# First query load on ScalarE's queue, six instead of nine leading zero products, the gate's "+1" on GpSimd, and a redrawn instruction order

## The chip, the cores and the metric

The kernel runs on one core of a Trainium2 chip. A core has a matrix engine (TensorE, PE in the profile), a vector engine (VectorE, DVE), a scalar engine with table functions (ScalarE, ACT), a general engine (GpSimd, POOL) and a queue engine that mostly issues transfers (SyncE, SP). Each runs its own list of instructions in order; they wait for each other by semaphores. ACT can issue transfers too. The metric is the device time of one execution in microseconds (us). Shorter is better.

## The reference

Two stages follow each other. The first is attention with soft-capped scores over 8 batches, 12 heads, 448 positions and 64 values per head:

```python
scores = scale * np.matmul(q, k.transpose(0, 1, 3, 2))
scores = cap * np.tanh(scores / cap)                     # cap = 30
attn = np.exp(scores - max);  attn /= attn.sum(-1)
x = (attn @ v)  ->  [8, 448, 768]
```

The second takes x (448 x 768 per batch) through a mixture of four attention experts, two of which are chosen for each position:

```python
logits = x @ w_gate;  topk = the two largest of four;  w = softmax of the two
for e in range(4):
    q, k, v = x @ wq[e], x @ wk[e], x @ wv[e]            # 64 wide each
    a = softmax(causal(scale * q @ k.T))
    out += (e in topk) * w_e * (a @ v @ wo[e])
```

Products run in float16 with float32 accumulation; inputs and the output are float32.

## The kernel before

The first stage goes by pairs of heads: 48 pairs p, six to a batch. For a pair, `load` (L471) brings q, k and v from memory: `kf` and `vf` (the first 384 positions), `qf` (all 448), and `ktf` and `vtf`, the last 64 positions, in two transfers of half a tile. The first two pairs are loaded one at a time, the later ones two at a time. `cast` (L618) turns them to float16: for pair 0 k on ACT, q on DVE and the rest on POOL. `tr` (L672) transposes q and k on PE and copies the result from a PSUM bank to `qk` (L695, L699 and L724 for pair 0, L715 for the others). `fill` (L764) makes the scores of one pair in three parts, Y1, X and Y2 (PE lines L752 and L762), into three X banks and two Y banks; `tanh` (L798, instruction at L805) reads each part on ACT, and `expo` (L811, L817) takes one exponential over the whole pair. `pv` (L821; L832 and L839) multiplies with v, DVE divides by the sums (L860, L863), and `xt` (L868) transposes the result into `xT`, the input of the second stage.

The second stage goes by batch, and its work is put between that of the pairs of the next batches: `b_v` (L939) makes v and the logits, `b_gate`, `b_gate1`, `b_gexp` and `b_gate2` (L999 to L1062) work out the gate on POOL and DVE, `b_qk` (L964) projects q and k, `b_mask` (L1064) spreads the choice of experts, `b_score` (L1093 to L1127) makes the expert scores in the X banks and their exponential on ACT (L1122), `b_pv`, `b_ot` and `b_wo` (L1162, L1193, L1222) finish the batch and store it. The last batch has an ending of its own (`last`, L1319; `last2`, L1467), in which many PSUM copies (`evac`, L375 and L381) may go to DVE or ACT. The gate's weights are e/(1+e) and 1/(1+e): `b_gexp` makes e on POOL, `b_gate2` adds 1 (L1056) and takes the reciprocal (L1057) on DVE, and POOL goes on.

The order on each engine is not the program's. `Graph.solve` (L132) is a list planner that runs before the kernel is built: it knows an assumed duration for each operation, a due time worked back from the fixed sequence of ACT (the tanh and exponential instructions), and due times given by hand (`due=(ref, t)`, t us after an ACT instruction). At each step it takes, on the engine that is free first, the ready operation with the least due time. In each 4 us of the plan a number from `SEEDS` (L23, 78 of them) shifts the due times by a pseudo-random amount of up to `JIT`/2. A transfer has an assumed time on the wire (`wire`).

At the start, PE has nothing to do until the first data come. `NWARM` (9) products of zeros, 512 columns each, are issued ahead (L1544), and `NFILL` (30) of 128 columns fill gaps. One small exponential on ACT (L1547) brings the table in early. In order, SP issues k and q of pair 0, k and q of pair 1, then the tails of pair 1, while ACT issues the two `ktf` transfers of pair 0. `tr_first_tails` (L718, L721) transposes pair 0's `ktf` part. Each transfer takes one of eight semaphores in turn, so that the ninth waits until the first has landed.

Of the kernel before, what the change touches and what calls it, by code (L numbers as in the profile page):

```python
# [10 lines left out]
AF = mybir.ActivationFunctionType  # L11
# [10 lines left out]
JIT = 0.549  # L22
SEEDS = (0, 277, 719, 88, 790, 157, 709, 606, 285, 730, 63, 826, 999, 577, 0, 998, 560, 424, 0, 0, 0, 0, 0, 618, 784, 951, 0, 460, 25, 911, 435, 331, 710, 235, 192, 243, 759, 815, 762, 59, 135, 842, 518, 725, 260, 0, 0, 0, 737, 833, 0, 852, 0, 951, 0, 877, 795, 0, 495, 199, 407, 374, 655, 0, 288, 645, 0, 0, 872, 410, 701, 204, 988, 494, 733, 571, 666, 645)  # L23
TWIRE = 0.1
BEGIN = {"POOL": 0.8, "DVE": 0.9, "SP": 0.8, "ACT": 0.8, "PE": 1.25}
NWARM = 9
KEEP = 8
# [3 lines left out]
KD = 34  # L31
NFILL = 30

# [18 lines left out]
class Graph:  # L52
# [79 lines left out]
    def solve(self, when, banks, lent):  # L132
# [44 lines left out]
        while len(order) < n:  # L177
            best = None
            for e, rs in ready.items():
                if not rs:  # L180
                    continue
                c = [(est(o, e), o) for o in rs if e == o.eng or not left]
                if not c:
                    continue
                t0 = min(x[0] for x in c)
                if t0 >= INF or (best is not None and t0 >= best[0]):
                    continue
                def rank(x):
                    u = x[1]
                    if u.name[:4] == "gexp":  # L190
                        return -INF, 0.0, 0
                    d = u.due + lag if u.first or left < TAIL else max(u.due + lag, t0 + 1.12)
                    d -= 0.211 * (u.grp is not None and not u.opens and left >= TAIL)
                    k = SEEDS[int(t0 / 4.0)] if t0 < 4.0 * len(SEEDS) else 0
                    if k:
                        d += ((u.idx * 40503 + k * 9973) % 1009 / 1009.0 - 0.5) * JIT
                    return d - 2.0 * (u.half == 1 and half == 1), u.due, u.idx

                near = t0 + (0.003 if left >= TAIL else SWITCH + 0.02)
                t, o = min((x for x in c if x[0] <= near), key=rank)  # L200
                early = e == "POOL" and t < HEAD
                if (e in ("PE", "DVE") or early) and not o.first:
                    for t2, u in c:
                        if u.first and u.due + lag < t + o.occ + 0.047 and t2 < t + (
                                o.occ if early else max(SWITCH + 0.01, min(o.occ, 0.25))):
                            t, o = t2, u
                            break
                if best is None or t < best[0]:
                    best = (t, e, o)
# [64 lines left out]
def kernel(  # L274
# [196 lines left out]
    def load(p, n):  # L471
# [13 lines left out]
        def tail(eng, dst, src, g):  # L485
# [3 lines left out]
        nc_eng = nc.sync  # L489
        sp(lambda: full(kf[s][:, d], k[b, h, 0:KM], KC), w=w("kf"), name=f"ldk{p}", wire=0.82 * n)  # L490
        sp(lambda: nc_eng.dma_start(qf[s][:, d], q[b, h].rearrange("h (p c) d -> p h (c d)", c=QC)),
           w=w("qf"), name=f"ldq{p}", wire=0.935 * n)

        def tail_(nm, t, src, z):
            eng, e = (nc.scalar, "ACT") if p == 0 and nm == "ktf" else (nc.sync, "SP")
            for g in range(2):
                sp(lambda g=g: tail(eng, t[s][:, dp], src, g), w=[(nm, x, g) for x in key],
                   r=[(z, s)], name=f"ld{nm[:2]}{p}", eng=e, wire=0.165 * n)

# [439 lines left out]
    def b_v(b, ref):  # L939
        x = b % 2  # L940
        for n in range(4):
            g = Group(AUX + XB, 1.8)
            w = WIN[n]
            for j0 in (0, 2, 4):
                def mm(g=g, w=w, j0=j0):
# [7 lines left out]
                   [("vps", b, n)], g, occ=0.22, name=f"v{b}_{n}",  # L953
                   due=(ref, 4.048 + 1.4 * n))
            lo = 64 if n == 3 else 0
# [8 lines left out]
    def b_qk(b, ref):  # L964
        x = b % 2
        for r in range(2):
            for which in "kq":
                g = Group(AUX + XB, 2.4)
                w2 = (wq2 if which == "q" else wk2)[r]
                for j in range(NDC):  # L970
                    def mm(g=g, w2=w2, j=j, which=which):
# [9 lines left out]
                        [(which, b, r)], g, name=f"{which}{b}_{r}",  # L981
                        due=(ref, 12.09 + 5.11 * r + 1.8 * (which == "q")))
                if which == "k":
# [61 lines left out]
    def b_gexp(b, m=4):  # L1045
        x = b % 2
        e = g_e[x][:, 0:m]
        g_(b, lambda: nc.gpsimd.tensor_tensor(e, eul[:, 0:m], e, ALU.pow), [(b, "e"), "eul"],
           ["e"], 1.05, 1.18)

    def b_gate2(b, m=4):
# [3 lines left out]
        e, w0 = g_e[x][:, w], g_w0[x][:, w]  # L1055
        dve(0.11, lambda: V.tensor_scalar_add(w0, e, 1.0), [(b, "e")], [(b, "w0")], lat=0.17)  # L1056
        dve(0.1, lambda: V.reciprocal(w0, w0), [(b, "w0")], [(b, "w0")], lat=0.18)  # L1057
# [484 lines left out]
    for i in range(NWARM + NFILL):  # L1542
# [3 lines left out]
            ["warmps"], gw, due=0.0 if i < NWARM else None, name="fill")  # L1546
    act(0.25, lambda: nc.scalar.activation(rcb[0], warm[:, 0:4].rearrange("p (n o) -> p n o", o=1),  # L1547
                                          AF.Exp), ["warm", "ident"], [("rcb", 0)])
    load(0, 1)
    load(1, 1)  # L1550
    for p in range(NPV):
# [13 lines left out]
        for what in order:  # L1565
            if what == "Y2" and p:
# [3 lines left out]
                pv(p - 1)  # L1570
                xt(p - 1, (ACTS["Y1", p], 4.601))
                if p % HP == 0 and p < NP:
# [15 lines left out]
                if p in exps:  # L1588
                    bb, s = exps[p]
                    b_pv(bb, s)  # L1590
                    if s == 1:
                        b_ot(bb)
                        b_wo(bb, ACTS["Y1", p], *((14.83, 1.8) if bb < LB - 1 else (10.566, 0.5)))
            fill(p, what)
# [68 lines left out]
```

## Time and profile before

| | |
|---|---|
| median of 3 runs | 310.02 us (309.29, 310.02, 310.08) |
| the profiled execution | 309.16 us, of it 307.4 us from its first to its last instruction |
| ACT busy | 290.8 us (95%) |
| PE busy | 280.5 us (91%) |
| DVE busy | 216.0 us (70%) |
| POOL busy | 181.4 us (59%) |
| first tanh (L805) on ACT begins at | 7.03 us |
| moved by transfers | 51.98 MB |

Rows of groups and of the timeline begin with the line of the kernel, engine, operation and tiles; `out<-in`, with partitions x elements. In a timeline the first number is the start in us from the beginning of the span, the second the time to the end of the last of the instructions that the row takes together (x3: three of them), and a bracket tells how long the engine was idle ahead of it and what released it. "SPq" and "ACTq" are the issue of a transfer by these engines; a transfer's "time to landing" counts from its issue.

### The profile page before, as it was taken

Reading aid. Unit: us, or ns where it says so; the run is one execution under the profiler, and the core shown is the slowest. Engines: PE = TensorE matmul, PEld = TensorE weight load, DVE = VectorE, ACT = ScalarE, POOL = GpSimd, SP = SyncE. Lnnn points to the kernel's source line nnn. Section 1 sums busy time; section 2 is a strip of 40 time slices with the busy share of each in tenths; the row PEclk is TensorE's granted clock in tenths of the full one; section 3 lists DMA queues with packets and bytes.
Section 4 is the critical chain, followed back from the end, with each engine's and each line's share of the span. In section 5 each row is a group of like instructions: output and inputs, shape, how many; then the busy total and the mean of one; then the engine's idle time right before and its main releaser. Section 6 shows DMA issues by size and latency. Waiting matters only on the chain.

```text
span 307.4 us, 8998 instructions
## 1 busy us (share of the span) xinstructions
PE 280.5 (91%) x3504; PEld 188.2 (61%) x3504; DVE 216.0 (70%) x660; ACT 290.8 (95%) x245; POOL 181.4 (59%) x502
## 2 busy tenths in 40 slices
PE   8787679999999999999999999999999989999992
PEld 4454446576655766667566676567665766577761
DVE  2363656477679867796866887787768765787882
ACT  3999999999999999999999999999999999999671
POOL 7883436499788572984649873946585413720320
PEclk9997999999999999999999999999999999999998
DMA  6997999899991798249975593186127600422136
GB/s 168 263 213 178 271 277 257 235 238 243 252 240 47 224 265 234 69 130 269 250 195 135 149 320 95 43 248 175 18 43 163 159 8 20 122 72 79 34 144 217
DMA packets 82075, 51.98 MB, mean 169 GB/s; under 512 B 42736, under 2 KB 78320, under 8 KB 82032
## 3 DMA queue, kind: packets, MB, share of 16 engines
q1 hardware_dynamic: 81728, 51.18, 63.7%
q8 instruction: 27, 0.44, 0.6%
q10 hardware_dynamic: 304, 0.23, 0.2%
q14 instruction: 16, 0.13, 0.1%
HBM read 36.19 MB, written 11.01 MB: 154 GB/s over the span
## 4 chain that ended last, share of the span: by engine, by line
PE 53%; ACT 30%; DVE 8%; POOL 5%; issue 2%; DMA 1%; DVEq 0%; ACTq 0%; POOLq 0%
ACT yp L805 15%; ACT yp L817 12%; PE A L974 7%; PE A L839 6%; PE Y L752 6%; PE A L947 4%; PE X L1113 4%; PE A L1234 4%; PE A L832 3%; PE A L1172 2%; PE A L878 2%; PE A L678 2%; DVE ob L381 2%; ACT pP L1122 2%; PE X L762 2%
## 5 line engine op out<-in xcount | busy, mean ns | idle before, releaser
L817 ACT ACTIVATE yp<-yp 128x3136 f16<-128x3136 f16 (+4 forms) x51 | 139.8, 2744 | 0.0
L805 ACT ACTIVATE yp<-Y 128x896 f16<-128x896 f32 (+2 forms) x100 | 96.2, 962 | 1.6 <-PE Y L752 1.6
L805 ACT ACTIVATE yp<-X 128x1344 f16<-128x1344 f32 (+2 forms) x50 | 65.9, 1318 | 0.1
L839 PE MATMUL A<-v,yp 128*128 128x65 f16 x1116 | 55.9, 194 | 0.0
L839 PEld LDWEIGHTS <-yp 128*128 128x128 f16 x1116 | 49.0, 98 | 4.9 <-issue 2.9
L832 PE MATMUL A<-vtz,yp 128*128 128x130 f16 x186 | 41.5, 223 | 10.0 <-ACT yp L817 5.4
L863 DVE TENSOR_TENSOR xk<-A,rca 128x256 f16<-128x256 f32 (+1 forms) x96 | 39.7, 415 | 2.8
L860 DVE RECIPROCAL rca<-A 128x4 f32<-128x4 f32 (+1 forms) x96 | 17.2, 179 | 25.6 <-PE A L839 24.1
L638 POOL CAST q<-qf 112x512 f16<-112x512 f32 x44 | 26.6, 613 | 13.6 <-DMA qf<-in_q_dram 6.6
L664 POOL CAST v<-vf 128x384 f16<-128x384 f32 x48 | 24.4, 514 | 11.2 <-PE A L839 7.1
L381 DVE COPY ob<-A 128x384 f32<-128x384 f32 (+1 forms) x52 | 28.1, 552 | 3.9 <-PE A L1234 2.8
L832 PEld LDWEIGHTS <-yp 128*128 128x128 f16 x186 | 18.1, 97 | 20.0 <-ACT yp L817 11.2
L1187 DVE SCALAR_TENSOR_TENSOR oB<-A,rcb,mw 128x256 f16<-128x256 f32 x54 | 25.3, 479 | 1.4
L715 DVE COPY qk<-A 128x960 f16<-128x960 f16 x33 | 21.0, 653 | 7.2 <-PE A L678 6.7
L752 PE MATMUL Y<-qk 64*128 64x448 f16 x136 | 24.9, 361 | 0.8 <-ACT yp L805 0.4
L1234 PE MATMUL A<-wo,oT 128*128 128x384 f16 x108 | 24.3, 326 | 0.8 <-DVE ob L381 0.3
L1197 POOL TENSOR_TENSOR oS<-oB,oB 128x512 f16<-128x512 f16 x14 | 16.1, 1153 | 14.4 <-DVE oB L1187 10.4
L1172 PE MATMUL A<-vB,pP 128*128 128x260 f16 x135 | 22.8, 274 | 1.0 <-DVE qk L715 0.7
L947 PE MATMUL A<-wvg,xT 128*128 128x260 f16 x168 | 23.0, 274 | 0.2
L678 PE MATMUL A<-ident,q 112*128 112x112 f16 x192 | 20.2, 212 | 2.3 <-DVE q L638 0.8
L623 POOL CAST k<-kf 128x384 f16<-128x384 f32 x33 | 16.6, 512 | 9.7 <-DMA kf<-in_k_dram 6.0
L887 DVE COPY xT<-A 128x448 f16<-128x448 f16 (+1 forms) x48 | 18.0, 377 | 4.8 <-PE A L878 4.5
(231 smaller groups left out, 587.3 us busy)
## 6 DMA issues: line engine op xcount, KB each, us to landing
qf<-in_q_dram SPq DMA_DIRECT2D x23, 448.0 KB, 6.3
kf<-in_k_dram SPq DMA_DIRECT2D x23, 384.0 KB, 5.7
vf<-in_v_dram SPq DMA_DIRECT2D x23, 384.0 KB, 5.1
out_dram<-ob SPq DMA_DIRECT2D x21, 384.0 KB, 3.3
ktf<-in_k_dram SPq DMA_DIRECT2D x46, 32.0 KB, 5.0
vtf<-in_v_dram SPq DMA_DIRECT2D x46, 32.0 KB, 4.5
out_dram<-ob SPq DMA_DIRECT2D x6, 192.0 KB, 3.3
ob<-in_moe_wv_dram SPq DMA_DIRECT2D x2, 384.0 KB, 5.0
```

The lines of the kernel that those rows point to most:

```text
L381: (nc.scalar.copy if o.eng == "ACT" else nc.vector.tensor_copy)(dst(), src())
L638: e(q16[i], qf[s][:, h].rearrange("p h (c d) -> p c h d", c=QC))
L678: nc.tensor.transpose(ps[:, 0:S].rearrange("m (g c t) -> m c g t", c=QC, t=16)[:, c], q16[i][:, c, :, :].rearrange("p h d -> p (h d)"), id ...
L752: nc.tensor.matmul(dst[:, g, o], kT[r, 128 * (c + 1) : 128 * (c + 2)], t[r, qs], start=True, stop=True,)
L805: ACTS[what, p] = act(c_act(n * (b - a)), lambda: nc.scalar.activation(y[:, a:b, 0:n], src[:, 0 : b - a, 0:n], AF.Tanh, scale=isc / capf), ...
L817: act(c_act(n * (b - a), False), lambda a=a, b=b, n=n: nc.scalar.activation(y[:, a:b, 0:n], y[:, a:b, 0:n], AF.Exp, scale=capf), ks, ks, f ...
L832: nc.tensor.matmul(ps[:, n, :, :], y[:, 2, w : w + 128], vtz[u], start=(n == 0), stop=False, skip_group_check=True,)
L839: nc.tensor.matmul(ps[:, n, h, :], y[:, SLOT[c][h], w : w + 128], v16[u][:, h, c, :], start=False, stop=(c == 2), skip_group_check=True,)
L863: dve(c_dve(128 * m), lambda g=g, i=i, rc=rc, m=m: nc.vector.tensor_tensor(xk[p % NXK][:, 2 * i : 2 * i + m, :, :], view(g)[:, 0:m, :, 0:D ...
L947: nc.tensor.matmul(bank(g)[:, 0 : E * Dh + E], xT[x][:, j, w : w + 128], wvg[:, j, :], start=(j == 0), stop=(j == NDC - 1),)
L1172: nc.tensor.matmul(bank(g)[:, 0 : E * (Dh + 1)], pB[pi][:, o : o + 128], vB[x][:, c, :, :], start=(t == 0), stop=(t == len(cs) - 1),)
L1234: nc.tensor.matmul(bank(g)[:, 0 : D // 2], oT[x][:, n // 2, r, n % 2, :], wo2[r][:, c0:c1], start=(r == 0), stop=(r == 1),)
```

## The change

Five things change, all of them in the text of the program; the planner then draws a new order for the whole kernel.

1. Pair 0's q is issued on ACT's queue; pair 0's two `ktf` transfers go from ACT's to SP's queue. The planner's assumed times on the wire for pair 0 are smaller.
2. 6 instead of 9 long zero products ahead, and 42 instead of 30 short ones. The small exponential at the start does not wait for `ident` any more, and its assumed duration is 1.5 us.
3. The "+1" of the gate goes from DVE to POOL.
4. Due times of the second stage's projections, of its output product and of `xt` change, and so do two small tolerances of the planner.
5. The 78 numbers in `SEEDS` are others.

```diff
-SEEDS = (0, 277, 719, 88, 790, 157, ...
+SEEDS = (0, 0, 719, 433, 75, 538, ...
...
-NWARM = 9
+NWARM = 6
...
-NFILL = 30
+NFILL = 42
...
-                near = t0 + (0.003 if left >= TAIL else SWITCH + 0.02)
+                near = t0 + (0.008 if left >= TAIL else SWITCH + 0.02)
...
-                        if u.first and u.due + lag < t + o.occ + 0.047 and t2 < t + (
+                        if u.first and u.due + lag < t + o.occ + 0.052 and t2 < t + (
...
-        sp(lambda: full(kf[s][:, d], k[b, h, 0:KM], KC), w=w("kf"), name=f"ldk{p}", wire=0.82 * n)
-        sp(lambda: nc_eng.dma_start(qf[s][:, d], q[b, h].rearrange("h (p c) d -> p h (c d)", c=QC)),
-           w=w("qf"), name=f"ldq{p}", wire=0.935 * n)
+        q_eng, qe = (nc.scalar, "ACT") if p == 0 else (nc.sync, "SP")
+        sp(lambda: full(kf[s][:, d], k[b, h, 0:KM], KC), w=w("kf"), name=f"ldk{p}",
+           wire=0.82 * n if p else 0.35)
+        sp(lambda: q_eng.dma_start(qf[s][:, d], q[b, h].rearrange("h (p c) d -> p h (c d)", c=QC)),
+           w=w("qf"), name=f"ldq{p}", wire=0.935 * n if p else 0.35, eng=qe)
...
-            eng, e = (nc.scalar, "ACT") if p == 0 and nm == "ktf" else (nc.sync, "SP")
             for g in range(2):
-                sp(lambda g=g: tail(eng, t[s][:, dp], src, g), w=[(nm, x, g) for x in key],
-                   r=[(z, s)], name=f"ld{nm[:2]}{p}", eng=e, wire=0.165 * n)
+                sp(lambda g=g: tail(nc.sync, t[s][:, dp], src, g), w=[(nm, x, g) for x in key],
+                   r=[(z, s)], name=f"ld{nm[:2]}{p}", wire=0.165 * n if p else 0.1)
...
-                   due=(ref, 4.048 + 1.4 * n))
+                   due=(ref, 4.367 + 1.4 * n))
...
-                        due=(ref, 12.09 + 5.11 * r + 1.8 * (which == "q")))
+                        due=(ref, 14.952 + 5.133 * r + 1.8 * (which == "q")))
...
+        g_(b, lambda: nc.gpsimd.tensor_scalar(g_w0[x][:, 0:m], e, 1.0, None, ALU.add), [(b, "e")],
+           ["w0"], 0.19, 0.34)
...
-        dve(0.11, lambda: V.tensor_scalar_add(w0, e, 1.0), [(b, "e")], [(b, "w0")], lat=0.17)
...
-    act(0.25, lambda: nc.scalar.activation(rcb[0], warm[:, 0:4].rearrange("p (n o) -> p n o", o=1),
-                                          AF.Exp), ["warm", "ident"], [("rcb", 0)])
+    act(1.5, lambda: nc.scalar.activation(rcb[0], warm[:, 0:4].rearrange("p (n o) -> p n o", o=1),
+                                          AF.Exp), ["warm"], [("rcb", 0)])
...
-                xt(p - 1, (ACTS["Y1", p], 4.601))
+                xt(p - 1, (ACTS["Y1", p], 4.838))
...
-                        b_wo(bb, ACTS["Y1", p], *((14.83, 1.8) if bb < LB - 1 else (10.566, 0.5)))
+                        b_wo(bb, ACTS["Y1", p], *((14.625, 1.8) if bb < LB - 1 else (10.566, 0.5)))
```

In the order that results, SP issues k of pair 0, the two `ktf` of pair 0, k and q of pair 1, the two `ktf` of pair 1, and then k and q of pairs 2 and 3 ahead of any v. On PE, pair 0's q transposes stand right behind its k transposes, and pair 0's `ktf` transpose (L721 before) stands behind both, with one more zero product between it and the first scores.

## The prediction

> **What bounds the kernel now.** I read the page first, then the busy time by stretches, then ACT's waits, and then the first ten and the last twenty us of the timeline.
>
> ```profile
> span 307.4 us, 8998 instructions
> PE 280.5 (91%) x3504; PEld 188.2 (61%) x3504; DVE 216.0 (70%) x660; ACT 290.8 (95%) x245; POOL 181.4 (59%) x502
> 0.00:7.03 7.03, 5.74 (x34) 2.75 (x34) 2.26 (x9) 2.41 (x4) 5.26 (x28) 1.00 0.61 166
> 7.03:286.00 278.97, 259.38 (x3286) 174.78 (x3285) 199.72 (x600) 277.80 (x216) 171.27 (x465) 0.99 0.66 171
> 286.00:307.40 21.40, 15.39 (x189) 10.65 (x186) 14.02 (x52) 10.58 (x26) 4.88 (x9) 0.95 0.42 142
> ACT yp L805 <- PE Y L752: 1.6, 2, 1.4
> ACT pP L1122 <- PE X L1113: 0.8, 2, 0.5
> ACT qB L381 <- PE X2s L1327: 1.8, 1, 1.8
> ACT pP L1385 <- PE A L1375: 1.5, 2, 1.2
> ```
>
> The rows of stretches give length, then busy time of PE, weight loads, DVE, ACT and POOL, the granted PE clock, the transfer engines' share and GB/s. There are three stages. In the head, 7.03 us, ACT waits for the first scores. In the middle, 278.97 us, ACT is busy for 277.80: only 1.17 us are idle, of which 0.2 (1.6 less the 1.4 of the first tanh) and 0.8 have a named cause. In the ending, 21.4 us, no engine is full. So a change that adds no work to ACT can win only from the head, from 1.17 us, and from the ending; it can lose anywhere. Head and middle add up: ACT's list is the same in both orders up to the ending.
>
> The head row by row:
>
> ```profile
> 0.79 1.20 ACTq L487 DMA_DIRECT2D ktf<-in_k_dram  x2
> 0.79 0.46 SPq L483 DMA_DIRECT2D kf<-in_k_dram  x1
> 1.25 3.59 PE L1544 MATMUL A<-warm 128*128 128x512 f16 x8 [1.25 <-DVE warm L507]
> 1.31 0.46 SPq L491 DMA_DIRECT2D qf<-in_q_dram  x1
> 2.02 1.28 ACT L1547 ACT_TABLE_LOAD   x1 [2.02 <-issue]
> 2.82 1.92 SPq L487 DMA_DIRECT2D ktf<-in_k_dram  x3
> 3.45 0.51 ACT L623 CAST k<-kf 128x384 f16<-128x384 f32 x1
> 4.32 0.43 DVE L638 CAST q<-qf 112x512 f16<-112x512 f32 x1 [1.89 <-DMA qf<-in_q_dram]
> 4.63 0.52 PE L688 MATMUL A<-ident,k 128*128 128x128 f16 x3
> 4.95 0.41 PE L1544 MATMUL A<-warm 128*128 128x512 f16 x1
> 5.06 0.29 POOL L659 CAST ktz<-ktf 128x128 f16<-128x128 f32 x1
> 5.41 0.23 PE L721 MATMUL A<-ident,ktz 128*128 128x128 f16 x1
> 5.71 0.36 PE L678 MATMUL A<-ident,q 112*128 112x112 f16 x4
> 5.91 0.72 PE L1544 MATMUL A<-warm 128*128 128x128 f16 x10
> 6.03 0.51 POOL L623 CAST k<-kf 128x384 f16<-128x384 f32 x1 [0.29 <-DMA kf<-in_k_dram]
> 6.63 0.36 PE L752 MATMUL Y<-qk 64*128 64x448 f16 x2
> 7.03 0.92 ACT L805 ACTIVATE yp<-Y 128x896 f16<-128x896 f32 x1 [1.37 <-PE Y L752]
> 7.94 0.66 DVE L715 COPY qk<-A 128x960 f16<-128x960 f16 x1 [0.97 <-PE A L678]
> 9.46 0.36 PE L752 MATMUL X<-qk 64*128 64x448 f16 x2
> 9.87 1.29 ACT L805 ACTIVATE yp<-X 128x1344 f16<-128x1344 f32 x1
> ```
>
> k is cast by 3.96 (3.45 + 0.51) and q by 4.75 (4.32 + 0.43), yet their transposes start on PE at 4.63 and 5.71. In between PE works off zero products (eight in 3.59 us, 0.449 each), and q's transposes stand behind the ninth and behind the `ktf` transpose at 5.41. From q's transposes to the first tanh it is 1.32 us (7.03 - 5.71).
>
> **The head's terms.** Six zero products end at 1.25 + 6 x 0.449 = 3.94, one short one brings it to about 4.05. If k lands as before, its transposes start there instead of at 4.63, and q's follow after the 0.31 to 0.35 that three transposes hold PE (0.52 less overlap): 4.40. q must be cast by then. Its issue moves from 1.31 to 0.79; the load took 3.0 us from issue to cast, so it lands at 3.8 and is cast at 4.23. It now goes beside k from the beginning, so the unfavourable end is no earlier landing at all: 4.32, cast at 4.75, transposes at 4.8. On ACT one issue (0.46 to 0.6) stands ahead of the table load instead of 1.20, so ACT is no later for k. Along this path the first tanh comes at 5.72 (4.40 + 1.32) to 6.12.
>
> What is late next is `ktf`. Its transposes still stand ahead of the first scores on PE, and its two transfers go from 0.79 on ACT to SP, behind k.
>
> ```profile
> qf<-in_q_dram SPq DMA_DIRECT2D x2, 224.0 KB, 3.6
> kf<-in_k_dram SPq DMA_DIRECT2D x2, 192.0 KB, 3.4
> ktf<-in_k_dram ACTq DMA_DIRECT2D x2, 16.0 KB, 3.2
> ktf<-in_k_dram SPq DMA_DIRECT2D x1, 16.0 KB, 3.8
> DMA to landing us min/median/max: 2.9/3.6/4.7
> ```
>
> The last number of a row is the median time to landing; the last row is for all `ktf` transfers of the first 16 us. SP issues them at 1.31 and, at 0.6 each (1.92 / 3, with a wait in it), 1.92. The later one lands between 1.92 + 2.9 = 4.8 and 1.92 + 3.8 = 5.7, and I take the middle, 5.3, since less traffic lies ahead of it than ahead of the 3.8. From there: cast 0.29, 0.06 to PE (5.35 to 5.41), about 0.25 for the transpose and one zero product, 0.40 to the tanh (6.63 to 7.03): 1.0 us. So the first tanh comes at 5.8 to 6.7; I take 6.3, a gain of 0.73 (0.3 to 1.2).
>
> Then pair 1 has to follow. Its first X tanh is 2.84 us behind the first tanh (9.87 - 7.03), so it would be wanted at 9.14. Its k, q and `ktf` are issued later, by two issues of 0.6 less the one of 0.5: 0.7. If the wire and not the issue sets their landing, nothing is lost (pair 0's k was cast 2.66 after its issue, so with a median of 3.4 pair 1's took about 4.2: it waited for the wire); if the whole 0.7 passes through, the copy at 7.94 ends at 9.3 instead of 8.60, and scores and tanh follow 0.8 later (about 0.4 for scores and 0.4 to ACT): 10.0, no gain. With the POOL cast of `ktf` also holding the k cast behind it (6.03 before, 6.1 to 6.8 now) I keep 0.5 of the 0.73, with ends 0 and 1.1. **Head: -0.5.**
>
> **Zero products.** The short ones only fill gaps; 12 more hold PE 0.07 each (0.72 / 10) where it is waiting: nothing while they stand ahead of work that isn't ready. If the data were early, the six ahead of pair 1's part would cost 0.4, and they are behind the first scores.
>
> A row bears on having fewer of them: the PE clock.
>
> ```profile
> 24.00:28.00 4.00, 2.28 (x29) 1.81 (x30) 0.61 (x2) 3.91 (x4) 1.48 (x5) 0.69 1.12 248
> ```
>
> Where PE did 2.28 us of work in 4, the granted clock went to 0.69. In the head it reads 1.00 throughout, in the stretch up to 7.03. With six long products PE may be idle for some tenths between 4.0 and 5.8; by these rows that costs nothing, since PE has idled longer at 1.00. A slow start is part of the second rival and priced there. The Trainium skill, TensorE: Matmul & The Clock Gate, Part 1, states that the clock is let up after about 3.4 us of sustained activity, in a window that runs freely; by that rule a broken first window would leave the first scores at half the clock, and the time would be the second rival's. The row at 24 us agrees that idleness lowers the clock; the head's rows don't show the start of it.
>
> **The gate.** The row of the removed DVE add and the nearest POOL rows:
>
> ```profile
> L1056 DVE TENSOR_SCALAR g_w<-g_e 128x4 f32<-128x4 f32 x7 | 2.7, 387 | 1.2 <-POOL g_e L1048 1.1
> L1027 POOL TENSOR_SCALAR ms<-g_r 128x16 f32<-128x16 f32 x14 | 3.3, 253 | 0.2
> ```
>
> The columns are busy time, mean ns of one, and the idle time before. DVE loses 7 x 0.39 = 2.7 us, POOL gains at most 7 x 0.25 = 1.8 us of its 181. Neither bounds the middle (70% and 59%). The reciprocal now waits in the add's place and 0.1 to 0.25 longer; what is queued behind it on DVE are copies of PSUM banks, for which PE waits. DVE's own wait here was 1.1 us, all of it in one of the seven batches. In the new order one masked q (L992) stands ahead of that wait. Between -0.5 and +0.25 in one place; I take 0.
>
> **The new order of the middle.** Per half pair, between score products into the Y banks, PE's instructions were counted and priced at columns / 2400 + 0.0025 us each (448 columns: 0.19; two such beside each other in the row at 6.63 take 0.36 with latency). Sums over the kernel agree, 233.27 and 233.29 us; the fullest pair holds 5.80 before and 5.75 after. The projections' due time is 2.86 us later, yet q of batch 0 ends half a pair later and batch 1's and 2's by one to two, while expert scores begin in the same half pair or the next. So PE isn't fuller. What can't be read from order is who waits by some tenths. The bounds are -0.94, if all named waits of 1.0 go save 0.06, and +2.4, if one expert exponential in each of seven batches waits the 0.48 of the longest (3.4, less 0.94). It is nearest to what is there, since durations and ACT's list stay: 0.
>
> **The ending.**
>
> ```profile
> 301.72 0.55 DVE L381 COPY kf<-X0s 128x384 f32<-128x384 f32 x1
> 301.90 0.48 ACT L381 COPY kf<-A 128x384 f32<-128x384 f32 x1 [0.50 <-PE A L1300]
> ```
>
> These are the two halves of the last block, side by side on two engines. In the new order both are on DVE, one behind the other: +0.44 (301.72 + 2 x 0.55 against 302.38). Against this two `ob` copies of the same shape and one copy of v leave DVE for ACT, and two small ones come to it: -2 x 0.55 + 0.55 = -0.55 in copies of this shape. Between the two ends I take +0.1; the two waits of 1.8 and 1.2 at its start stay, since the products that they wait for stand at the same places.
>
> **Sum.** 309.16 - 0.5 + 0 + 0 + 0.1 = 308.76 against the profiled execution. That one lies below all three timed runs, and 0.86 below their median; the mean of the four is 309.64, and -0.4 from there is 309.2. I say 309.1, since the head may keep all of its 0.73. The runs of one kernel scatter by 0.8 us here; 0.3% (0.93 us) is about what a measurement of this kernel can tell from no change.
>
> **Rivals.** (1) The order also takes the waits out of the middle: 309.1 - 0.94 = 308.2. For it: the named waits are few; ahead of the longest, PE has about 0.3 us less to do in the new order. Against: nothing in the text aims at these three places. (2) The head's gain is lost on the way, by `ktf` and pair 1's loads landing late, or by a slow PE clock: ten transposes and five score products at half the clock add about 0.5 + 0.3 between the first tanh and pair 1. The time is then that of before with the ending's 0.1: 309.7. For it: the 0.7 later issue. Against: pair 1's copy at 8.60 had 0.8 until its scores. (3) Slower: expert scores come late. Its place is the X banks in each batch (L1113), its point the moment at which q's masked copies are done later than the ACT slot; later due times move that way. If every second of the fourteen waits 0.48, that is 3.4, so 309.1 + 3.4 - 0.94 = 311.6; with half of them 310.4, and I put 311.0. Against: the half-pair counts.
>
> **Chances.** Forecast 0.50 (308.5 to 309.8 by itself, of which nearly half is below 309.09, the 0.3% bound); rival 1 0.16; rival 2 0.16; rival 3 0.18. Faster: 0.24 + 0.16 + 0.02 = 0.42; same: 0.26 + 0.14 = 0.40; slower 0.18. The range leaves out about 0.05 below and 0.12 above: 308.1 to 310.8.
>
> **What would show it.** Right: the first tanh at 6.0 to 6.6, q's cast at about 3.8 to 4.3, the `ktf` cast on POOL after 4.8 directly ahead of the first scores, pair 1's X tanh at 9.1 to 9.7, ACT idle in the middle near 1.2 us, and the last copy on DVE at about 0.5 ahead of the end of copies before. Wrong: a first tanh after 6.8 (`ktf`), before 5.8 (it wasn't on the path), ACT waits for L1113 of more than 2 us, or transfer waits on POOL of 3 us and more in the 20 to 50 us in which transfers are full.

## The result and the profile after

The changed kernel takes 310.55 us (median of 21 runs, 309.55 to 311.47); the kernel before, run beside it, 309.88 (21 runs, 309.00 to 310.39). The ratio is 1.0024, with a 95% interval of 1.0013 to 1.0035: slower by 0.67 us, where 309.1 was predicted. That lies inside the predicted range, but it is a loss where a gain of 0.8 was forecast (309.1 for 309.88). The profiled run of the changed kernel took 311.4, near the slowest of its 21; that of before 309.16, near its fastest. So the two profiles are 2.2 us apart and the medians 0.67: the profiles name the mechanisms, and their sizes are taken from medians below.

First the lines at the top of the page of the changed kernel.

```profile
span 309.7 us, 9017 instructions
PE 281.0 (91%) x3513; PEld 191.3 (62%) x3513; DVE 214.3 (69%) x653; ACT 290.4 (94%) x245; POOL 182.8 (59%) x509
```

ACT's busy time is nearly the same (290.8 before), so the 2.3 us of span are time in which it waits. Three cuts place them: the beginning of pair 1's X tanh, the end of ACT's last large exponential, the end. Busy time by these stretches (columns as in the prediction), for the kernel before,

```profile
0.00:9.87 9.87, 8.53 (x65) 4.50 (x66) 2.91 (x10) 5.25 (x8) 7.63 (x41) 1.00 0.70 198
9.87:286.67 276.80, 257.26 (x3264) 173.64 (x3264) 199.69 (x602) 275.63 (x214) 169.14 (x454) 0.99 0.66 170
286.67:307.40 20.73, 14.72 (x178) 10.04 (x175) 13.38 (x49) 9.91 (x26) 4.64 (x9) 0.95 0.44 147
```

and for the changed one:

```profile
0.00:11.99 11.99, 9.46 (x62) 5.23 (x62) 2.98 (x10) 5.54 (x7) 6.61 (x35) 1.00 0.77 179
11.99:288.37 276.38, 256.63 (x3279) 176.01 (x3278) 198.36 (x595) 275.17 (x213) 171.55 (x467) 1.00 0.69 169
288.37:309.70 21.33, 14.90 (x176) 10.04 (x174) 12.93 (x49) 9.68 (x26) 4.66 (x9) 0.95 0.42 143
```

Head +2.12, middle -0.42, ending +0.60: together the 2.30 of span (these cuts go by spans printed to a tenth; the ending is good to 0.05). In the middle ACT is idle for 1.21 us (276.38 less 275.17), as before for 1.17 (276.80 less 275.63), but 1.0 of it in one place, L1124, and 0.2 ahead of one Y tanh, where before 0.48, 0.28 and 0.18 were in three places; the 0.42 are in its busy time, 275.17 for 275.63, and so are not waits that went. The wait that is new stands ahead of pair 1's X tanh (ACT's waits, in all, times, longest):

```profile
ACT yp L806 <- PE X L763: 1.3, 1, 1.3
ACT pP L1124 <- PE X L1115: 1.0, 1, 1.0
```

The head, in the timeline of the changed kernel:

```profile
4.61 0.43 DVE L639 CAST q<-qf 112x512 f16<-112x512 f32 x1 [2.18 <-DMA qf<-in_q_dram]
4.81 0.51 ACT L624 CAST k<-kf 128x384 f16<-128x384 f32 x1 [2.06 <-DMA kf<-in_k_dram]
5.30 0.29 POOL L660 CAST ktz<-ktf 128x128 f16<-128x128 f32 x1 [1.16 <-DMA ktf<-in_k_dram]
5.38 0.50 PE L689 MATMUL A<-ident,k 128*128 128x128 f16 x3 [1.29 <-ACT k L624]
6.75 0.55 PE L753 MATMUL Y<-qk 64*128 64x448 f16 x2
7.35 0.92 ACT L806 ACTIVATE yp<-Y 128x896 f16<-128x896 f32 x1 [0.96 <-PE Y L753]
8.39 0.85 PE L1546 MATMUL A<-warm 128*128 128x128 f16 x6
9.17 0.55 PE L753 MATMUL Y<-qk 64*128 64x448 f16 x2
10.46 0.66 DVE L716 COPY qk<-A 128x960 f16<-128x960 f16 x1 [2.91 <-PE A L679]
11.30 0.36 PE L753 MATMUL X<-qk 64*128 64x448 f16 x2
11.99 1.29 ACT L806 ACTIVATE yp<-X 128x1344 f16<-128x1344 f32 x1 [1.31 <-PE X L763]
12.53 0.50 PE L1546 MATMUL A<-warm 128*128 128x128 f16 x6
```

Two things differ from before. Pair 0's k is cast at 4.81 instead of 3.45; PE, out of zero products at 4.09, stood still for 1.29. And PE is slow: two products of 448 columns take 0.55 at 6.75 and at 9.17, and only from 11.30 on the 0.36 that the first scores took before (6.63 there). It is about half speed: six products of 128 columns take 0.85 at 8.39 and three 0.53 at 8.07, so three more cost 0.32; from 12.36 on three take 0.33 and six 0.50, and three more cost 0.17. Pair 1's copy, which stands behind these products, comes at 10.46 instead of 7.94. The clock's column (third from the end) shows nothing of it: it reads 1.00 over the whole of that time.

```profile
6.00:9.00 3.00, 3.00 (x23) 1.79 (x21) 1.08 (x3) 2.04 (x3) 2.21 (x12) 1.00 0.89 217
9.00:12.00 3.00, 3.00 (x31) 1.93 (x28) 0.66 (x1) 1.42 (x3) 0.81 (x3) 1.00 1.08 221
```

The column is a default there. The trace's list of clock records begins only where the clock rises, at 10.52 us in the changed kernel and at 5.00 in the kernel before; for the time ahead of its first record the trace has no clock, and the column counts that as full. So the rise can be read from the trace after all, and it fits the durations.

The ending. The last copies and stores of the changed kernel:

```profile
303.09 0.56 DVE L381 COPY kf<-X0s 128x384 f32<-128x384 f32 x1
303.56 0.55 DVE L381 COPY kf<-A 128x384 f32<-128x384 f32 x1
303.80 1.22 SPq L1318 DMA_DIRECT2D out_dram<-kf  x2
```

Measured from the end of the last large exponential, the last copy ends at 15.74 (303.56 + 0.55 - 288.37), before at 15.71 (301.90 + 0.48 - 286.67). Both halves on DVE cost 0.03, not 0.44, since PE's last product ends 0.18 earlier. The 0.6 arise behind all engines, in the transfers. Their share by half microseconds, at the end of before and of the changed kernel (the last two columns are the share of the 16 transfer engines and GB/s):

```profile
305.40:305.90 0.50, 0.00 (x0) 0.00 (x0) 0.00 (x0) 0.00 (x0) 0.00 (x0) 0.50 0.65 258
305.90:306.40 0.50, 0.00 (x0) 0.00 (x0) 0.00 (x0) 0.00 (x0) 0.00 (x0) 0.50 0.00 0
```

```profile
306.70:307.20 0.50, 0.00 (x0) 0.00 (x0) 0.00 (x0) 0.00 (x0) 0.00 (x0) 1.00 0.80 301
307.20:307.70 0.50, 0.00 (x0) 0.00 (x0) 0.00 (x0) 0.00 (x0) 0.00 (x0) 0.78 0.07 25
307.70:308.20 0.50, 0.00 (x0) 0.00 (x0) 0.00 (x0) 0.00 (x0) 0.00 (x0) 0.50 0.05 18
```

Before, all engines stop together. After, a share of 0.05 to 0.07, that is about one of sixteen, goes on alone for about 0.8 us. The view of queues for the last 4 us has a row in the changed kernel that before has not:

```profile
q14 instruction: 1, 0.01, 0.5%
```

One packet of instructions, 0.01 MB, lies 3.2 us ahead of the end among the last stores. In the kernel before, the last such packet lies 8.3 us ahead. That the engine which goes on alone is the one that carried the packet is not recorded.

### The profile page after: what moved, and what is told of

It reads as the page before. It is cut to its first block, busy times and chain, and to the rows that moved or that the text cites. A ratio compares the mean times of both kernels' runs of the same rounds, so it can differ in the third digit from the quotient of the medians.

```text
span 309.7 us, 9017 instructions
## 1 busy us (share of the span) xinstructions
PE 281.0 (91%) x3513; PEld 191.3 (62%) x3513; DVE 214.3 (69%) x653; ACT 290.4 (94%) x245; POOL 182.8 (59%) x509
## 4 chain that ended last, share of the span: by engine, by line
ACT 67%; PE 13%; DMA 6%; POOL 5%; DVE 4%; issue 3%; DVEq 0%; POOLq 0%
ACT yp L806 34%; ACT yp L818 29%; ACT pP L1124 4%; DMA mT<-mB 3%; PE A L948 2%; DMA kd<-kz 1%; DMA kf<-in_k_dram 1%; DVE qm L993 1%; POOL mB L1071 1%; POOL oS L1199 1%; PE Y L753 1%; DVE ob L381 1%; PE A L1546 1%; PE A L840 1%; PE A L1329 1%
## 5 line engine op out<-in xcount | busy, mean ns | idle before, releaser
L818 ACT ACTIVATE yp<-yp 128x3136 f16<-128x3136 f16 (+4 forms) x51 | 142.5, 2797 | 0.0
L806 ACT ACTIVATE yp<-Y 128x896 f16<-128x896 f32 (+2 forms) x100 | 102.0, 1020 | 1.4 <-PE Y L753 1.4
L806 ACT ACTIVATE yp<-X 128x1344 f16<-128x1344 f32 (+2 forms) x50 | 68.7, 1375 | 1.3 <-PE X L763 1.3
L381 DVE COPY ob<-A 128x384 f32<-128x384 f32 (+1 forms) x50 | 26.9, 553 | 3.0 <-PE A L1236 2.2
L1236 PE MATMUL A<-wo,oT 128*128 128x384 f16 x108 | 25.0, 326 | 1.8 <-DVE ob L381 0.8
L948 PE MATMUL A<-wvg,xT 128*128 128x260 f16 x168 | 21.2, 273 | 0.3 <-DVE xT L888 0.3
L1134 POOL TENSOR_SCALAR_AFFINE_SELECT pP<-pP 128x384 f16<-128x384 f16 x14 | 7.4, 525 | 22.5 <-ACT pP L1124 13.3
```

The source lines that it names most:

```text
L381: (nc.scalar.copy if o.eng == "ACT" else nc.vector.tensor_copy)(dst(), src())
L806: ACTS[what, p] = act(c_act(n * (b - a)), lambda: nc.scalar.activation(y[:, a:b, 0:n], src[:, 0 : b - a, 0:n], AF.Tanh, scale=isc / capf), ...
L818: act(c_act(n * (b - a), False), lambda a=a, b=b, n=n: nc.scalar.activation(y[:, a:b, 0:n], y[:, a:b, 0:n], AF.Exp, scale=capf), ks, ks, f ...
L948: nc.tensor.matmul(bank(g)[:, 0 : E * Dh + E], xT[x][:, j, w : w + 128], wvg[:, j, :], start=(j == 0), stop=(j == NDC - 1),)
L1236: nc.tensor.matmul(bank(g)[:, 0 : D // 2], oT[x][:, n // 2, r, n % 2, :], wo2[r][:, c0:c1], start=(r == 0), stop=(r == 1),)
```

## The experiments

Five theories. (1) The new queues make pair 0's k land late. (2) Six long zero products leave PE at half its clock through the head. (4) The ending's 0.6 is that packet of instructions, and its place hangs on how many instructions an engine has (4a: DVE). (5a) The gate's move is free. (3) was that the head is not the cause at all. In every experiment the planner is as it was and only what is emitted differs, so all other orders stay. The kernel before, run beside each group of them, had medians of 309.50 to 309.69, and 309.88 in the first comparison, so a difference of medians across groups is good to some tenths.

**The queues and the zero products, one at a time.**

```
e1   pair 0: k, q on SP; ktf x2 on ACT          (changed kernel, old queues, 6 long)
e2   pair 0: ktf, k, ktf on SP; q on ACT        (kernel before, nearly the new queues, 9 long)
e3   6 -> 9 long zero products, ahead of all    (changed kernel, new queues)
e4   9 -> 6 long zero products, first 3 out     (kernel before, old queues)
```

In e2 one `ktf` is issued ahead of k, which is neither the changed kernel's order nor that of the expectation below: k is issued at 1.43 instead of 0.79, so part of its late landing there is its late issue.

> The changed kernel with the first two `ktf` transfers back on ACT's queue ahead of its table load, and the first q back on SP behind k, as in the kernel before; six long zero products, everything else and every order stay. Theory 1 (k lands late because of the queues): k is cast at about 3.5 instead of 4.81, its transposes start at about 4.1 instead of 5.38, the first tanh at 6.0 to 6.7, pair 1's X tanh at 9.7 to 10.3 instead of 11.99, and the time is 0.5 to 0.9 below the changed kernel's: 309.7 to 310.1. Theory 2 (six long zero products leave PE at half its clock, whatever the queues): products of 448 columns still take 0.55 instead of 0.36 up to about 10 us, pair 1's X tanh stays at 11 or later, and the time stays at 310.3 to 310.6. Theory 3 (the head is not it, the ending's 0.6 is): 310.3 to 310.6 with pair 1's X tanh early.

> The kernel before with the changed kernel's queues alone: the first q on ACT's queue, and on SP k, then the two `ktf` transfers, then pair 1's. Nine long zero products, all orders as before. Theory 1: k is cast at 4.5 or later instead of 3.45, the first tanh at 7.2 to 7.6, pair 1's X tanh at 10.5 to 12 instead of 9.87: 0.6 to 2.0 slower, 310.5 to 311.9. Theory 2: the ninth zero product covers the gap up to 5.2, PE stays at full clock (0.36 for 448 columns), and the time is within 0.3 of before: 309.6 to 310.2.

> The changed kernel with nine long zero products instead of six, three more ahead of all the others; nothing else. Theory 1: nothing changes, since k still lands late: k's transposes at about 5.4, first tanh at 7.3, 310.4 to 310.7. Theory 2: PE comes to full clock before the first scores (0.36 for 448 columns instead of 0.55), pair 1's X tanh at 10.0 to 10.7 instead of 11.99, and the time falls by 0.7 to 1.5: 309.0 to 309.8.

> The kernel before with six long zero products instead of nine (the first three left out); nothing else. Theory 1 as the only cause: k's transposes start at about 4.0 instead of 4.63, the first tanh comes at 6.2 to 6.6 instead of 7.03 and the time falls by 0.3 to 0.7: 309.2 to 309.6. Theory 2: with PE idle between the zero products and the transposes the clock stays at half, 448 columns take 0.55 up to about 10 us, pair 1's X tanh comes at 10.5 to 12 instead of 9.87, and the time rises by 0.5 to 2.0: 310.4 to 311.9.

| run | median (range) | ratio to before, 95% | k cast | first tanh | X tanh, pair 1 |
|---|---|---|---|---|---|
| e1 | 309.26 (308.51 to 311.17) | 1.0004 [0.9984, 1.0023] | 3.51 | 6.60 | 11.61 |
| e2 | 311.96 (309.49 to 314.17) | 1.0062 [1.0042, 1.0081] | 4.42 | 7.21 | 10.04 |
| e3 | 309.53 (309.17 to 309.85) | 0.9993 [0.9985, 1.0002] | 4.62 | 7.14 | 10.36 |
| e4 | 311.25 (310.07 to 311.98) | 1.0047 [1.0028, 1.0065] | 3.67 | 8.41 | 12.19 |

Theory 2 is borne out twice. Three more long zero products, and nothing else, take 1.02 off the changed kernel (310.55 to 309.53; by the ratios to the kernel before, 1.0024 and 0.9993, it is 0.96) and narrow its runs from 1.9 us to 0.7; three fewer cost the kernel before 1.7 (its X tanh, at 12.19, is 0.2 beyond the expected range). Theory 3 falls with that. Theory 1 is right in its mechanism: with the old queues k is cast at 3.51 and 3.67, with the new at 4.62 (e3). What e1's time says is split: its median is 1.29 below the changed kernel's, lower than either theory expected, but its runs fall into two groups, seven at 308.5 to 309.4 and five at 310.2 to 311.2, and the profiled one is of the upper. In that one the old queues buy nothing, since the clock is slow (timeline, and the row of a stretch):

```profile
3.51 0.51 ACT L624 CAST k<-kf 128x384 f16<-128x384 f32 x1
4.07 0.50 PE L689 MATMUL A<-ident,k 128*128 128x128 f16 x3
6.00 0.56 PE L753 MATMUL Y<-qk 64*128 64x448 f16 x2
8.42 0.56 PE L753 MATMUL Y<-qk 64*128 64x448 f16 x2
11.61 1.29 ACT L806 ACTIVATE yp<-X 128x1344 f16<-128x1344 f32 x1 [1.68 <-PE X L763]
3.90:7.26 3.36, 3.13 (x20) 1.28 (x19) 1.70 (x4) 1.26 (x3) 1.89 (x9) 1.00 0.81 222
```

The first tanh was 0.75 earlier than in the changed kernel's profile, and the X tanh of pair 1 still came at 11.61: the gain of the head as the prediction had worked it out was there (6.60, against 6.3 taken), and PE's half clock ate it before pair 1. PE was busy for 3.13 of 3.36 us in that stretch, and the clock rose only at 10.53.

e2 lies just above what theory 1 expected, but not by its mechanism: its X tanh, at 10.04, is only 0.17 late, and the loss is behind. Pair 2's q is cast late too, PE runs dry in one stretch and is at half clock through the next (the issue of k, a row of the timeline, two stretches with the clock in the third column from the end, and, for the second loss, a row of the timeline and one of DVE's waits):

```profile
1.43 0.58 SPq L483 DMA_DIRECT2D kf<-in_k_dram  x1
12.76 0.90 DVE L638 CAST q<-qf 112x512 f16<-112x512 f32 x2 [3.98 <-DMA qf<-in_q_dram]
11.20:14.60 3.40, 1.78 (x17) 0.92 (x17) 1.27 (x3) 3.40 (x3) 2.20 (x15) 0.99 1.01 267
14.60:18.00 3.40, 3.27 (x35) 2.13 (x33) 1.64 (x6) 2.45 (x3) 3.03 (x17) 0.51 1.00 232
275.45 1.02 ACT L1122 ACTIVATE pP<-X 128x1024 f16<-128x1024 f32 x1 [1.96 <-PE X L1113]
DVE qm L992 <- DMA mT<-mB: 1.9, 1, 1.9
```

That costs ACT about 1 us; another 1.5 (1.96 against 0.48 before) is lost at 275.45, behind a masked q that waited for a transfer. Why that transfer was late there was not tried.

**Which of q and `ktf` holds k back, and how many zero products it takes.** a1 puts the two `ktf` behind q on ACT's queue in e3. b1 is e1 with eight long zero products.

> The changed kernel with nine long zero products (309.53, k cast at 4.62 after a wait of 1.86 for its transfer) and with the first two `ktf` transfers on ACT's queue behind q, so that SP has k and then pair 1's loads and only q, not `ktf`, is issued beside k. If it is `ktf`'s small packets right behind k on the same queue that hold k back: k is cast at about 3.5, and k's transposes start as soon as the long zero products end (5.2). If it is q beside k that takes its share of the wire: k stays at 4.4 to 4.8. Since nine long zero products hold PE to 5.2 anyway, the time hardly moves in either case: 309.2 to 309.8, with `ktf` (cast at 5.3 to 6.0) setting the first tanh.

> The changed kernel with the old queues for pair 0 (its runs with six zero products fell into two groups, 308.5 to 309.4 and 310.2 to 311.2, and the profiled one, of the upper group, had PE at half clock up to 10.6) and with eight long zero products instead of six. Theory 2, in the form that the clock comes up at the end of a stretch of about 3.4 us in which PE had no pause: two more long products close the pauses ahead of the first scores, the clock is up by about 7 in every run, and the upper group goes: 308.5 to 309.2 with a scatter under 1 us, X tanh of pair 1 at 9.4 to 10.2. If the two groups have another cause than PE's pauses (transfers that land late), they stay, and the median lies at 309.3 to 310.0.

a1: 309.96 (309.76 to 310.32), 0.4 above e3 and just above what was expected, which is not explained; k is cast at 4.47 although no `ktf` of pair 0 stood on SP. So it is q beside k, not `ktf` behind it; the 4.28 to 4.81 of all seven profiles with q on ACT's queue stand against 3.41 to 3.67 of all ten without. b1: 309.09 (308.85 to 311.66), with k cast at 3.41, scores at 0.36 from 6.15 on and the X tanh at 9.79. Of eleven runs one was above 310, of e1's twelve five; that one, 311.66, is outside the scatter of 1 us that was expected. By medians b1 is 0.44 below e3, by the ratios to the kernel before (0.9998 and 0.9993) it is not: what the old queues are worth beside a full warm-up is not clear of the noise.

**The same kernel again, and one lucky profile.** Three more profiles of e1 (r1, r2, r3), and the changed kernel with seven memsets on DVE that nobody reads, c2, made for the ending.

```
+  for _ in range(7): nc.vector.memset(pad, 0.0)     ahead of DVE's first cast of q
```

> A second look at the changed kernel with the old queues and six long zero products, whose runs fell into two groups. If the groups are the clock's: a time of 308.5 to 309.4 goes with products of 448 columns at 0.36 from about 6.3 on and pair 1's X tanh at 9.3 to 10.0; a time of 310.2 to 311.2 goes with 0.55 up to 10 and an X tanh at 11.5 or later, as in the first profile.

> A third look at the changed kernel with the old queues and six long zero products. A time of 308.5 to 309.4 must go with products of 448 columns at 0.36 before 8 and pair 1's X tanh at 9.3 to 10.2, if the groups are the clock's; with 0.55 up to 10 it must be 310.2 to 311.2. A time of the lower group with the slow clock would refute it.

> As the look before: 308.5 to 309.4 with 0.36 before 8 and an X tanh at 9.3 to 10.2, or 310.2 to 311.2 with 0.55 up to 10.

> The changed kernel with nothing but the seven memsets on DVE. If the ending's part adds to the head's as it did with nine and with eight long zero products (0.68 and 0.64 less): 309.8 to 310.0 instead of 310.55, ending 20.5 after the last exponential, the slow clock up to 10 and the late X tanh (11 to 12) as they were.

r1, r2, r3 took 311.04, 310.84 and 310.56, with 0.55 to 0.60 for two products of 448 columns up to 8.6 and the X tanh at 11.69, 11.20 and 11.46: the upper time with the slow clock, as expected, each time. The lower time was not among them. c2 shows the other state, against what was expected of it. Its head is that of the changed kernel, with six long products and the new queues, and the memsets beside it on DVE:

```profile
4.43 0.51 ACT L624 CAST k<-kf 128x384 f16<-128x384 f32 x1 [1.67 <-DMA kf<-in_k_dram]
4.99 0.34 PE L689 MATMUL A<-ident,k 128*128 128x128 f16 x3 [0.90 <-ACT k L624]
6.40 0.36 PE L753 MATMUL Y<-qk 64*128 64x448 f16 x2
10.10 1.29 ACT L806 ACTIVATE yp<-X 128x1344 f16<-128x1344 f32 x1 [0.38 <-PE X L763]
```

PE stood still for 0.90 here too, yet at 4.99 it is at full speed, three transposes in 0.34 instead of 0.50, and the X tanh comes at 10.10. So nearly the same head has its clock up at 4.08 in one execution and at 10.52 in another, by the first clock record of each trace. Of the seven profiles with six long products one has the rise at 4.08 and six at 9.67 to 10.64; the ten with eight or nine have it at 4.30 to 6.95, that is no later than in the first X scores. By the profiles, then, half clock up to about 10 is usual with six and does not come with eight or nine. How often it comes in the timed runs is not known, since they have no trace; if e1's lower group is the fast clock, it is the more frequent one there. c2's runs, 309.63 (308.38 to 310.69), are 2.3 us wide, those of e1 2.7; those of e3 and p2 below, with nine long products, 0.7 and 0.9. Width alone does not tell the clock: b1, g3 and e2, with eight or nine, are 2.8 to 4.7 wide.

The Trainium skill, TensorE: Matmul & The Clock Gate, Part 1, says that the clock is set by a window of about 3.4 us that runs freely, and so differs from run to run; the trace agrees, with the 3.40 us at 0.51 in e2 and with the two outcomes above. In the clock records the windows can be counted: stretches at half clock in mid-kernel are 3.41 us long, those at full clock whole multiples of that (6.83 in e1, 20.48 before, 296.96 in the changed kernel). Counted back from the rise, c2's window held the six long products, and the changed kernel's, two windows ahead of its rise, did not hold all of them (c2, then the changed kernel):

```profile
0.66:4.08 3.42, 2.84 (x7) 0.89 (x7) 1.18 (x12) 1.49 (x2) 2.75 (x14) 1.00 0.57 135
0.28:3.69 3.41, 2.45 (x6) 0.89 (x7) 0.82 (x5) 1.49 (x2) 2.60 (x16) 1.00 0.42 95
```

So with six products it is the place of the window that decides. But e1's next window, from 3.70 to 7.11, had PE busy for 3.18 and was not enough. Part 4 of the same page of the Trainium skill states that transposes do not count as busy in the same way, which would fit: 1.34 us of e1's window are transposes (eight, from 4.07 to 5.97). Without the transposes the windows sort in all 17 traces: PE was busy for at most 2.58 us where the clock then stayed down and for at least 2.82 in the window at whose end it rose. No run here takes the transposes away.

**The gate.** g3 is e3 with the seven sums back on DVE, b2 is b1 with the same, g2 is the kernel before with the sums on POOL.

```
g3, b2   - nc.gpsimd.tensor_scalar(g_w0[x][:, 0:m], e, 1.0, None, ALU.add)
         + nc.vector.tensor_scalar_add(g_w0[x][:, 0:m], e, 1.0)
g2       the reverse, in the kernel before
```

> The changed kernel with nine long zero products and the gate's seven sums back on DVE, no order changed otherwise: this is the price of the gate's move, against 309.53. Theory 5a: the move costs nothing in the middle, 309.3 to 309.7. Theory 4 about the ending (one transfer of instructions falls 3.2 ahead of the end in all three profiles of the changed order, and 8.4 ahead in those of the old one, and behind it one of the 16 transfer engines finishes the last stores alone, about 0.6 later than the others): if the place of that transfer hangs on DVE's or POOL's count of instructions (7 more on DVE and 7 fewer on POOL, as in the kernel before), it moves away, the ending falls from 21.34 to about 20.75 after the last exponential, and the time is 308.8 to 309.1. If it stays, the count that matters is another engine's or the order's.

> Old queues, eight long zero products and the gate's sums on DVE, all on the changed order: the sum of the two runs beside it. If the head's and the ending's parts add up: the head's gain of the old queues and the ending without the late transfer engine, 307.9 to 308.6; if the ending stays, as the run with eight alone, 308.5 to 309.2.

> The kernel before with the gate's seven sums on POOL, no order changed otherwise: the gate's part alone, in the old order. In the changed order, taking the sums back to DVE cost 1.5 in the median, because DVE then waited 2.1 for POOL there and ACT behind it. In the old order DVE's wait was 1.1, and the reciprocal behind the sum needs the same data, so the wait stays: the middle within 0.3 of 276.80. Theory 4a: with 7 fewer instructions on DVE the transfer of instructions moves from 8.4 to about 3 ahead of the end and the ending grows from 20.73 to 21.2 or more: 310.0 to 310.3 in all. Otherwise 309.4 to 309.9.

g3: 311.06 (310.23 to 314.57), ratio 1.0065 [1.0038, 1.0091], that is 1.5 above e3. b2: 311.93, 2.8 above b1. g2: 308.85 (308.33 to 309.08), ratio 0.9976 [0.9966, 0.9987], 0.65 below before. None of the three times came as expected. Theory 5a falls in both orders: the gate's move is worth 0.65 in the old order and 1.5 to 2.8 in the new, the ending's part below included. Waits in the middle of g3's profile, of DVE and of ACT (in all, times, longest):

```profile
DVE g_w L1051 <- POOL g_e L1049: 2.1, 3, 1.2
ACT yp L806 <- PE Y L753: 3.6, 3, 1.9
```

With the sum on DVE, DVE waits for POOL in three batches; the copies of PSUM banks stand behind it, PE waits for the banks and ACT for PE. In e3 ACT has no such wait for Y in its middle. The profiled run of g3 is one of its slowest, 313.86, and shows why its runs are so far apart: behind the longest of DVE's waits PE stands still for 2.11 us, so that it is busy for 1.30 of 3.41, and the next 3.41 are at half clock,

```profile
165.46:168.87 3.41, 1.30 (x8) 0.55 (x6) 2.86 (x4) 3.41 (x4) 2.41 (x7) 1.00 1.11 320
168.87:172.29 3.42, 3.42 (x34) 2.13 (x33) 1.92 (x6) 2.62 (x3) 0.59 (x3) 0.50 0.72 255
```

and two of ACT's three waits for Y, 0.80 and 1.87, follow at 171 and 175. In the profile of b2, its fastest run (310.63), the clock stays up and the waits for Y come to 1.2. In g2 the middle is 275.99 instead of 276.80. Of ACT's three waits there in the kernel before (0.18, 0.28, 0.48) one is left; the other two are 0.46 of the 0.81:

```profile
ACT pP L1122 <- PE X L1113: 0.5, 1, 0.5
```

**The ending.** p1 is b1, and p2 is e3, with the seven memsets.

> Old queues and eight long zero products on the changed order (309.09 without more), and seven memsets of a scratch tile that nobody reads on DVE ahead of its first cast, where DVE is idle. Gate and orders as in the changed kernel. Theory 4a (the late transfer of instructions hangs on DVE's count of instructions): it moves from 3.2 to about 7.0 ahead of the end, the ending falls from 21.3 to about 20.4 after the last exponential, the middle stays at 276.4 to 277.0, and the time is 308.1 to 308.5, below both kernels. If it hangs on POOL's count, everything stays: 308.9 to 309.3.

> The same seven memsets on the changed kernel with nine long zero products and its new queues (309.53 without them). Theory 4a: 308.5 to 308.9, ending 20.4. Otherwise 309.3 to 309.8, ending 21.3.

p1: 308.45 (307.61 to 309.14), ratio 0.9961 [0.9947, 0.9975]. p2: 308.85 (308.09 to 309.01), ratio 0.9974 [0.9964, 0.9984]. Both came as expected. These are 0.64 and 0.68 below the same kernels without the memsets. c2 is 0.92 below the changed kernel, but its runs mix both states of the clock. The memsets take 0.82 us where DVE is idle:

```profile
2.38 0.82 DVE L1635 MEMSET pad<- 128x2 uint32 x7
```

The time from the last large exponential to the end sorts all profiles: 20.7 to 20.9 in the old order, 21.3 to 21.4 in the eight of the changed order with its own gate, 20.5 in the five with seven more instructions on DVE, memsets or gate sums. In those five the packet lies 6.9 ahead of the end instead of 3.2, in g2, with seven fewer on DVE, 5.7 instead of 8.3. Theory 4a holds in that DVE's number of instructions moves the packet, in both directions, and that the packet's place is worth 0.64 to 0.68 here. It missed by how far in g2: about 3 and an ending of 21.2 or more were expected, and at 5.7 the ending stayed at 20.9. p1 beats both kernels, by 1.05 and 2.1; of the change it has the orders and the gate, with the old queues, eight long zero products and the memsets.

## Why the prediction was wrong, step by step

- **"If k lands as before, its transposes start there" failed.** q was sent on a second queue beside k, and the step asked only whether q would land earlier. k's cast went from 3.45 to 4.81 in the profile, 4.28 to 4.81 over the runs, and a1 shows that q is what it shares with. q gained less than k lost: its cast began at 4.61 in the profile, beyond the unfavourable end, 4.32, and at 3.76 to 4.61 over the seven profiles with q on ACT's queue, against 4.29 to 4.61 in the ten without. `ktf` came at 5.30, as taken.
- **"By these rows that costs nothing, since PE has idled longer at 1.00" failed, and it is the largest term:** +1.02 in the median (e3), +1.7 in the old order (e4). The step trusted the column of the granted clock in the head. The durations quoted with it said otherwise: 0.449 for a zero product of 512 columns and 0.52 for three transposes in the first 5 us, where the same three take 0.33 later on, in this row of the kernel before:

```profile
7.32 0.33 PE L688 MATMUL A<-ident,k 128*128 128x128 f16 x3
```

  That was a slow clock under a column of 1.00, and the column is 1.00 there only because the trace has no clock record ahead of the rise, at 5.00 in that profile. So PE had not idled at full clock in the head, and six products were often too few to bring the clock up.
- **The way to the first tanh came out late.** 6.3 was taken, with 5.8 and 6.7 as ends. The profile had 7.35, by k and the clock and not by `ktf`, and all profiles with the new queues 6.62 to 7.35; with the old queues and six long products on the new order it came at 6.60 to 6.76. And the first tanh was not what counted: pair 1's X tanh was, 2.84 behind it before and 4.64 behind it after.
- **The second rival had the mechanism**, late loads of pair 1 and a slow clock, with a chance of 0.16, and too low a price: 0.8 for the slow clock, where the X tanh moved by 2.12 in the profile. It priced fifteen instructions and not the way of pair 1's q transposes on PE, which stand behind two more score products in the new order. By the Trainium skill's rule, which the prediction quoted and set aside, the time was that rival's, 309.7, where 310.55 was measured; the rule was right on what happens in the profiled runs, and the size was the prediction's own.
- **The gate, 0 (-0.5 to +0.25), was mis-sized:** -0.65 in the old order. The wait of 1.1 was on the page. The step held that the reciprocal takes the add's place in it; it did not ask whether ACT stood at the end of that queue.
- **The middle, 0, measured -0.42** in the profile, with ACT's idle time unchanged at 1.2; the third rival's waits at L1113 (L1115 in the changed kernel) came once (1.0 us at one place, in place of 0.8 at two), not in every batch, and the first rival's gain, all waits gone, did not come. Why ACT's instructions were 0.46 shorter in all is not explained. The third rival's "with half of them 310.4" does not follow from its own terms, 309.1 + 1.7 - 0.94 = 309.9; nothing hangs on it.
- **The ending, +0.1, measured +0.60.** Its own step, the two copies behind each other, cost 0.03. The term that counted, a packet of instructions among the last stores, was not in the sum.
- The terms together: +1.0 (zero products, e3), +0.4 (queues, e3 against b1, not clear of the noise), +0.6 (ending, from the profiles), -0.65 (gate in the old order) make +1.35, where +0.67 was measured. The rest, -0.7, is in the orders of head and middle and in terms that don't add, such as a gate that is worth more in the new order; no run separates it, and it stays open.

## What to carry to other kernels

Read PE's speed at the start from the durations of equal products, since the clock's column says 1.00 also where the trace has no record, and do not shorten a warm-up to start earlier unless the work behind it keeps PE full; and price a head by when the steady rhythm begins, not by its first result. A transfer that is moved to start earlier takes from the one it now runs beside: ask for both. Where a kernel ends in stores, see whether a packet of instructions falls among them, and move it by a few idle instructions.

## What the runs showed of the hardware that was not expected

- In the changed kernel's first 10.5 us products run at about half speed (0.55 against 0.36 for two of 448 columns), and the column of the granted clock reads 1.00 for want of a record. Later on the column does show it (0.51 in e2's stretch of 3.40 us, after one in which PE was busy for 1.78 of 3.40).
- 2.84 us of zero products in a window of 3.41 us brought the clock up, 2.45 did not, and 3.18 us of which 1.34 were transposes did not either.
- With one packet of instructions among the last stores, one of sixteen transfer engines was busy for about 0.8 us longer than the others; seven more small instructions on DVE moved the packet by 3.7 us and saved 0.64 and 0.68.
- Seven sums of 128x4, 2.7 us of DVE in all, were worth 0.65 to 2.8 of the kernel's time by where they waited, not by their length.
